# Attention loads on ScalarE's DMA queue, and the last projections tied to the last product

## The chip, the cores and the metric

The kernel runs on one core of a Trainium2 chip. The metric is the device time of one execution in microseconds (us). An execution with the profiler gives the trace that is read here; it shows the engines TensorE (PE; its weight loads are PEld), VectorE (DVE), ScalarE (ACT), GpSimd (POOL) and SyncE (SP). A name with a q behind it, as SPq, is the engine's sequencer, which issues DMAs and waits for semaphores.

## What is computed

Linear attention over 8 batches and 8 heads of 576 rows of 64, then a gated feed-forward layer over the 4608 rows of 512 that come out of it. Inputs and outputs are float32.

```
q_s = softmax of q over its 64 columns
k_s = softmax of k over the 576 rows
kv  = k_s^T v                 per batch and head, 64 x 64
x   = q_s kv                  heads side by side: 4608 x 512
out = ((x @ w_a) * (x @ w_b)) @ w_out     w_a, w_b: 512 x 1536, w_out: 1536 x 512
```

## The kernel before

The 4608 rows are cut into nine chunks of 512 (`T`), numbered `c`. While the feed-forward layer of one chunk runs on TensorE, the attention of the next chunk is done beside it. The program is written in an order that a scheduler then changes: it places each engine's instructions by its own estimate of when they can run, within their dependences. `tc.issue_after(ins)` holds the instructions of a block behind `ins`, where they run on the same engine. On the chip each engine then takes its instructions strictly in order, each waiting for its semaphores; a DMA is issued by an instruction in the order of the engine that issues it, so a DMA that must wait holds up whatever stands behind it there.

The feed-forward layer of a chunk has six steps `i` (`NI`). In each, seven products of 12 matmuls (128x256 outputs, helper `product`) go into the PSUM tiles `kx`, `ky`, `ka` and `kp`: a scheme with seven instead of eight block products, so that some tiles are accumulated on after they have been read. `ky` and `kp` share one bank (tag `k1`), so the product into `kp` must wait until VectorE has read `ky`. ScalarE copies `kx` to `u` (L692), VectorE adds `ky` to it (L693), `ka` after that (L695), and so on, until the gated values `cc` stand there. `g_split` makes two float32r halves of them: ScalarE casts the high one, `gh` (L79), VectorE subtracts for the low one, `gl` (L82). Two such pairs come out of a step, `gh0`/`gl0` and `gh1`/`gl1`, one for each of the twelve (`NF`) parts `f` of w_out. A projection (`project`, L468) multiplies a pair with `wo[f]`: 12 matmuls with 128x512 outputs into the four PSUM tiles `po`. Projections stand in the list `pend` and are run a step later, by `run_pending`, between the products. After the last of a chunk, `store` copies the four `po` tiles to `ot` and sends them out.

The weights of the products come back from DRAM for every chunk after the first two: `get_w` loads `ws` tiles (L165, 512 KB each, eight buffers). The attention of a chunk needs these loads: `k` (L189), `v` (L195), `q` (L277); and, for chunks from 2 on, where q is taken in twice, once for its statistics and once turned, `qtt` (L344) and twice `mr` (L347). `mr` holds the statistics of q, broadcast over partitions; they are written to DRAM as `dq` (L338) and read back. With both there, VectorE adds `mr` to `qtt` (L354), ScalarE takes the exponential (L355) and casts `qh` (L79), VectorE makes `ql` (L82), TensorE multiplies them with `kvh` and `kvl` into `px` (L381), and VectorE multiplies `px` with the other half of `mr` into `xf` (L559). `mr` has two buffers, so the load for the third of four groups waits for that last step of the first.

All DMAs are issued by SyncE. ScalarE issues none. The last lines of the program are

```
    while pend:
        run_pending()
```

and they run the projections that are still open after the last step of the last chunk.

Of the kernel before, what the change touches and what calls it, by code (L numbers as in the profile page):

```python
# [23 lines left out]
A11, S2, S3, S1, A12, S4, A22 = range(7)  # L24
B11, T2, T3, T1, B21, B22, T4 = range(7)
# [4 lines left out]
def linear_attention_then_gated_ffn(  # L30
# [18 lines left out]
    nc = tc.nc  # L49
    B, NP, P, J, _, D = k.shape  # L50
# [3 lines left out]
    NF = 2 * NI  # L54
    T = 512
    H = T // 2
    TT = T // P
    NCH = NT // T
    LATE = NCH - qt_late.shape[0]
# [25 lines left out]
    wo = {}  # L85
# [45 lines left out]
    def split_wo(f):  # L131
        split(wo[f][:, 0], wo[f][:, 1], wo[f][:, 1].bitcast(F32))
# [5 lines left out]
    def split_w(y):  # L138
        w = ws_tile()
        yv = y.rearrange("p (n c f) -> p n c f", n=2, c=2)  # L140
        split(w[:, :, 0], w[:, :, 1], yv)
        return w
# [20 lines left out]
    def get_w(i, op):  # L163
        w = ws_tile()
        nc.sync.dma_start(out=w.bitcast(F32), in_=dw[i, op].bitcast(F32))  # L165
        return w
# [19 lines left out]
    def k_load(b, g, kt=None):  # L186
        if kt is None:
            kt = sb.tile([P, J, 2, D], F32, name="kt")
        nc.sync.dma_start(out=kt, in_=k[b, g])  # L189
        return kt  # L190

    def v_load(b, g, vt=None):
        if vt is None:
            vt = sb.tile([P, J, 2, D + 1], F32, name="vt")
        nc.sync.dma_start(out=vt, in_=v[b, g])  # L195
        return vt

    def kv_soft(b, kt, tags=("at", "at")):
# [75 lines left out]
    def q_load(c, g, qt=None):  # L274
        if qt is None:
            qt = sb.tile([P, TT, 2, D], F32, name="qt")
        nc.sync.dma_start(out=qt, in_=q[c, g])  # L277
        return qt

    def q_soft_first(qt):  # L280
# [60 lines left out]
    def q_turned(c, g, dq):  # L341

        qt = sb.tile([P, T], F32, name="qtt", tag="kt")
        nc.sync.dma_start(out=qt, in_=qt_late[c - LATE, g])  # L344
        mr = sb.tile([P, 2, T], F32, name="mr", bufs=2)
        for h in range(2):
            nc.sync.dma_start(  # L347
                out=mr[h * D:(h + 1) * D].rearrange("d w t -> d (w t)"),
                in_=dq[g, h].unsqueeze(0).broadcast_to([D, 2 * T]),
            )  # L350
        return qt, mr
# [33 lines left out]
    def xo_tile(shape):  # L385
        return sb.tile(shape, F32R, name="xo", bufs=11)
# [56 lines left out]
    def product(pt, w, x, first):  # L443

        for n in range(2):
            i = 0
            for c in range(2):
                for wp, xp in ((0, 0), (0, 1), (1, 0)):
                    nc.tensor.matmul(  # L449
                        pt[:, n], w[:, n, wp, c], x[:, xp, c],  # L450
                        start=(first and n == 0 and i == 0), stop=(i == 5),
                        skip_group_check=True,
                    )
                    i += 1

    def project_first(f, g, po):
        for t in range(TT):
            nc.tensor.matmul(
                po[t], g[:, t * P:(t + 1) * P], wo[f][:, 1].bitcast(F32),
                start=(f == 0), stop=(f == NF - 1),  # L460
            )

    def project(f, ghl, po):
        gh, gl = ghl
        for t in range(TT):
            ts = slice(t * P, (t + 1) * P)
            for i, (a, w) in enumerate(((gh, 0), (gh, 1), (gl, 0))):
                nc.tensor.matmul(  # L468
                    po[t], a[:, ts], wo[f][:, w],
                    start=(f == 0 and i == 0), stop=(f == NF - 1 and i == 2),  # L470
                )

    def store(c, po):
        for t in range(TT):
            ot = sb.tile([P, DM], F32, name="ot", tag="wr", bufs=4)
            if c == NCH - 1:
                nc.scalar.copy(out=ot[:, 0:H], in_=po[t][:, 0:H])
                nc.vector.tensor_copy(out=ot[:, H:], in_=po[t][:, H:])
            else:
                nc.scalar.copy(out=ot, in_=po[t])  # L480
            nc.sync.dma_start(out=out[c * T + t * P:c * T + (t + 1) * P, :], in_=ot)
# [108 lines left out]
    for g in range(NP):  # L590
        kt = const.tile([P, J, P], F32, name=f"kt_first{g}", tag=f"wo{NF - 1 - g}")
        vt = const.tile([P, J, 2, D + 1], F32, name=f"vt_first{g}", tag=f"wo{NF - 5 - g}")
        qt = qts[:, g].rearrange("p n (j h d) -> p (n j) h d", h=2, d=D)
# [14 lines left out]
    for g in range(NP):  # L608
        kt, vt, qt = first[g]
        odd = g % 2  # L610
        kt = kv_soft_t(kt, (("at", "k0"), ("k1", "k2"))[odd])
# [7 lines left out]
        x = xo_tile([P, 2, T])  # L619
# [11 lines left out]
    po = [ps.tile([P, DM], F32, name=f"po{t}") for t in range(TT)]  # L631
    pending = None
    for f in range(NF):
# [10 lines left out]
        ghl = gate_first(f, x0)  # L644
# [3 lines left out]
    pend = [(pending[0], pending[1], 0, po)]  # L648

    def run_pending(last_only=False):  # L650

        if not pend:
            return
        f, ghl, c, po = pend.pop(0)
        (project if c else project_first)(f, ghl, po)
        if f == NF - 1:
            store(c, po)

    last = None
    for c in range(1, NCH):  # L660
        more = c + 1 < NCH
        attend = Spread(attention_tasks(c + 1) if more else [], 3 * NI - 3 - (1 if c == 1 else 0))
        po = None
        x, xo = xo, {}
        for i in range(NI):
            def operand(op):
                if c > 1:
                    return get_w(i, op)
                if op in (A11, A12, A22):
                    return get_w(i, op)  # L670
                w = split_w(sy[i][op])
                put_w(i, op, w)
                return w

            if more and i == NI - 1:
                x_operands(xfs[c + 1], early, xo)
            kx = ps.tile([P, 2, H], F32, name="kx", tag="k0")
            ky = ps.tile([P, 2, H], F32, name="ky", tag="k1")
            ka = ps.tile([P, 2, H], F32, name="ka", tag="k2")
            cc = sb.tile([P, 4, 2, H], F32, name="cc", bufs=1)  # L680
            u2 = sb.tile([P, 2, H], F32, name="u2", bufs=1)
            u3 = sb.tile([P, 2, H], F32, name="u3", bufs=1)
            if c > 1 or i > 0:
                attend(last)
            if c == 1:
                if i + 1 < NI:
                    sy[i + 1] = sums(i + 1)
                split_wo(2 * i)
                split_wo(2 * i + 1)
            product(kx, operand(A11), x[B11], True)  # L690
            product(ky, operand(S2), x[T2], True)
            nc.scalar.copy(out=u2, in_=kx)  # L692
            nc.vector.tensor_tensor(out=u2, in0=ky, in1=u2, op=ALU.add)  # L693
            product(ka, operand(S3), x[T3], True)
            last = nc.vector.tensor_tensor(out=u3, in0=ka, in1=u2, op=ALU.add)  # L695
            if more and i == NI - 1:
                x_operands(xfs[c + 1], late, xo)
            end = c == NCH - 1 and i == NI - 1
            if not end:
                run_pending()  # L700
            attend(last)
            kp = ps.tile([P, 2, H], F32, name="kp", tag="k1")
            product(kp, operand(S1), x[T1], True)
            product(kx, operand(A12), x[B21], False)

            nc.vector.tensor_tensor(out=cc[:, 3], in0=kp, in1=u3, op=ALU.add)  # L706
            nc.scalar.copy(out=cc[:, 0, 0], in_=kx[:, 0])  # L707
            nc.vector.tensor_tensor(out=cc[:, 0, 0], in0=kx[:, 1], in1=cc[:, 0, 0], op=ALU.mult)
            last = nc.vector.tensor_tensor(out=cc[:, 3, 0], in0=cc[:, 3, 0], in1=cc[:, 3, 1], op=ALU.mult)
            if not end:  # L710
                run_pending()
            if po is None:
                po = [ps.tile([P, DM], F32, name=f"po{t}") for t in range(TT)]
            attend(last)
            product(kp, operand(S4), x[B22], False)
            nc.vector.tensor_tensor(out=cc[:, 1], in0=kp, in1=u2, op=ALU.add)  # L716
            nc.vector.tensor_tensor(out=cc[:, 1, 0], in0=cc[:, 1, 0], in1=cc[:, 1, 1], op=ALU.mult)  # L717
            g1 = g_split(2 * i, cc[:, 0:2, 0])
            product(ka, operand(A22), x[T4], False)
            nc.vector.tensor_tensor(out=cc[:, 2], in0=ka, in1=u2, op=ALU.add)  # L720
            last = nc.vector.tensor_tensor(out=cc[:, 2, 0], in0=cc[:, 2, 0], in1=cc[:, 2, 1], op=ALU.mult)
            g2 = g_split(2 * i + 1, cc[:, 2:4, 0])
            pend += [(2 * i, g1, c, po), (2 * i + 1, g2, c, po)]
    while pend:
        run_pending()


# [48 lines left out]
```

## Time and profile before

| | |
|---|---|
| median of 3 runs | 991.0 us (990.97 to 994.56) |
| the profiled execution | 986.57 us, span from first to last instruction 984.5 us |
| mean granted TensorE clock | 0.99 |
| busy: TensorE, its weight loads | 948.7 us (96%), 854.0 us (87%) |
| busy: VectorE, ScalarE, GpSimd | 632.5 (64%), 391.7 (40%), 112.8 us (11%) |
| DMA queue that SyncE issues on | 93600 packets, 282.57 MB, 81.9% of 16 engines' time |
| HBM | read 241.40 MB, written 37.98 MB |

Busy time of TensorE is from each matmul's start to its modelled end. A row of the order of time has its start (us), its length (us), engine, line, operation, tiles and sizes, and in brackets how long the engine had stood idle before it and what released it. Lines are those of the kernel before.

### The profile page before, as it was taken

What the parts mean: (1) busy time and instruction counts of PE and PEld (TensorE: products, weight loads), DVE (VectorE), ACT (ScalarE), POOL (GpSimd) and SP (SyncE); (2) the same over time, 40 slices, a digit from 0 to 9 for tenths busy, and PEclk for the clock granted to TensorE, in tenths of its full rate; (3) what the DMA queues carried; (4) which work ended last, traced back from release to release, by engine and by line L of the source; (5) the groups of instructions that cost most, each with busy time, mean ns of one, the idle gap of its engine ahead of it and who ended that gap; (6) DMA issues with size and microseconds to landing.
All of it is one profiled execution on the core that took longest, in us unless ns stands there. A gap on an engine that the chain in (4) does not pass through costs nothing.

```text
span 984.5 us, 16997 instructions
## 1 busy us (share of the span) xinstructions
PE 948.7 (96%) x6171; PEld 854.0 (87%) x6171; DVE 632.5 (64%) x1259; ACT 391.7 (40%) x1087; POOL 112.8 (11%) x96
## 2 busy tenths in 40 slices
PE   3889999999999999999999999999999999999998
PEld 3757666899999999999999999999999999899996
DVE  7797786988686665656566657565656545653443
ACT  8666675542372325322442335223532263221111
POOL 3245344531000000000000000000000000000000
PEclk9799999999999999999999999999999999999999
DMA  9699858999989967997699779977998679767761
GB/s 346 228 412 397 340 207 293 358 332 303 307 279 338 321 241 280 334 334 259 240 339 328 267 258 341 320 264 252 337 295 295 232 282 288 269 230 262 256 212 46
DMA packets 93682, 283.64 MB, mean 288 GB/s; under 512 B 10848, under 2 KB 11424, under 8 KB 93600
## 3 DMA queue, kind: packets, MB, share of 16 engines
q1 hardware_dynamic: 93600, 282.57, 81.9%
q8 instruction: 49, 0.80, 0.3%
q14 instruction: 33, 0.27, 0.1%
HBM read 241.40 MB, written 37.98 MB: 284 GB/s over the span
## 4 chain that ended last, share of the span: by engine, by line
PE 70%; DMA 6%; DVE 2%; ACT 1%; issue 1%; SPq 0%; DVEq 0%
PE po L468 24%; PE kp L449 12%; PE ka L449 12%; PE kx L449 12%; PE ky L449 6%; DMA mr<-dq 4%; DMA qtt<-in_q_late 2%; PE pk L251 2%; PE px L381 2%; DMA dq<-sst 1%; DVE ws L82 0%; ACT qt L323 0%; SPq L347 0%; DVE ql L82 0%; ACT gh L79 0%
## 5 line engine op out<-in xcount | busy, mean ns | idle before, releaser
L468 PE MATMUL po<-wo_w,gh 128*128 128x512 f32 x768 | 226.5, 394 | 1.0 <-ACT gh L79 1.0
L449 PE MATMUL kx<-xo,ws 128*128 128x256 f32 x1152 | 164.8, 284 | 0.0
L449 PE MATMUL ka<-xo,ws 128*128 128x256 f32 x1152 | 163.1, 285 | 0.9 <-DVE cc L720 0.7
L468 PEld LDWEIGHTS po<-wo_w,gh 128*128 128x128 f32 x768 | 138.8, 189 | 27.3 <-ACT gh L79 1.4
L449 PE MATMUL kp<-xo,ws 128*128 128x256 f32 x1152 | 158.3, 284 | 1.1 <-DVE u L693 1.0
L449 PEld LDWEIGHTS ka<-xo,ws 128*128 128x128 f32 x1152 | 152.1, 192 | 4.5 <-DVE cc L720 0.9
L449 PEld LDWEIGHTS kx<-xo,ws 128*128 128x128 f32 x1152 | 151.9, 191 | 3.5 <-issue 0.5
L449 PEld LDWEIGHTS kp<-xo,ws 128*128 128x128 f32 x1152 | 148.2, 191 | 3.9 <-DVE u L693 1.2
L468 PE MATMUL po<-wo_w,gl 128*128 128x512 f32 x384 | 136.9, 395 | 0.0
L79 ACT CAST gh<-cc 128x512 fp32r<-128x512 f32 x96 | 57.6, 620 | 147.4 <-DVE cc L717 144.1
L716 DVE TENSOR_TENSOR cc<-kp,u 128x512 f32<-128x512 f32 x48 | 33.0, 688 | 89.1 <-PE kp L449 88.8
L323 ACT ACTIVATE qt<-qt,st 128x64 f32<-128x64 f32 x224 | 75.0, 336 | 34.7 <-DVE st L320 30.5
L468 PEld LDWEIGHTS po<-wo_w,gl 128*128 128x128 f32 x384 | 71.2, 188 | 15.3
L449 PE MATMUL ky<-xo,ws 128*128 128x256 f32 x576 | 78.5, 285 | 2.5 <-ACT xo L79 2.1
L426 PE MATMUL pt<-xo,ws 128*128 128x512 f32 x288 | 76.1, 415 | 3.0 <-ACT ga L433 3.0
L449 PEld LDWEIGHTS ky<-xo,ws 128*128 128x128 f32 x576 | 72.9, 192 | 3.2 <-ACT xo L79 2.4
L82 DVE TENSOR_TENSOR gl<-cc,gh 128x512 fp32r<-128x512 f32 x96 | 66.9, 704 | 9.6 <-ACT gh L79 9.4
L426 PEld LDWEIGHTS pt<-xo,ws 128*128 128x128 f32 x288 | 55.0, 194 | 19.3 <-ACT ga L433 4.0
L707 ACT COPY cc<-kx 128x256 f32<-128x256 f32 x48 | 17.7, 370 | 130.8 <-PE kx L449 122.1
L706 DVE TENSOR_TENSOR cc<-kp,u 128x512 f32<-128x512 f32 x48 | 32.9, 685 | 54.8 <-PE kp L449 54.8
L219 POOL PARTITION_ALL_REDUCE mx<-m x20 | 14.1, 704 | 467.2 <-DVE m L205 435.4
L355 ACT ACTIVATE qtt<-qtt 128x512 f32<-128x512 f32 x28 | 17.7, 633 | 103.9 <-DVE qtt L354 77.4
(127 smaller groups left out, 1241.8 us busy)
## 6 DMA issues: line engine op xcount, KB each, us to landing
ws<-dw SPq DMA_DIRECT2D x312, 512.0 KB, 5.2
dw<-ws SPq DMA_DIRECT2D x42, 512.0 KB, 5.0
mr<-dq SPq DMA_DIRECT2D x56, 256.0 KB, 6.5
raw<-in_w_ab SPq DMA_DIRECT2D x24, 512.0 KB, 7.9
out<-ot SPq DMA_DIRECT2D x36, 256.0 KB, 4.8
vt<-in_v SPq DMA_DIRECT2D x28, 325.0 KB, 7.3
qt<-in_q SPq DMA_DIRECT2D x32, 256.0 KB, 5.2
kt<-in_k SPq DMA_DIRECT2D x24, 320.0 KB, 5.8
```

Source lines behind the costliest of these rows:

```text
L79: nc.scalar.copy(out=hi, in_=src)
L82: nc.vector.tensor_tensor(out=lo, in0=src, in1=hi.bitcast(F32), op=ALU.subtract)
L251: nc.tensor.matmul(pk, kt[:, j].rearrange("p h d -> p (h d)"), vt[:, j], start=(j == 0), stop=(j == J - 1),)
L323: nc.scalar.activation(out=qt[:, j, h], in_=qt[:, j, h], func=AF.Exp, bias=st[:, h, 0, j:j + 1], accum_out=st[:, h, 1, j:j + 1],)
L355: nc.scalar.activation(out=qt, in_=qt, func=AF.Exp)
L381: nc.tensor.matmul(px[:, s], w, m[:, s], start=(i == 0), stop=(i == 2))
L426: nc.tensor.matmul(pt, w[:, wp], x[g][:, xp], start=(i == 0), stop=(i == 3 * NP - 1))
L449: nc.tensor.matmul(pt[:, n], w[:, n, wp, c], x[:, xp, c], start=(first and n == 0 and i == 0), stop=(i == 5), skip_group_check=True,)
L468: nc.tensor.matmul(po[t], a[:, ts], wo[f][:, w], start=(f == 0 and i == 0), stop=(f == NF - 1 and i == 2),)
L706: nc.vector.tensor_tensor(out=cc[:, 3], in0=kp, in1=u3, op=ALU.add)
L707: nc.scalar.copy(out=cc[:, 0, 0], in_=kx[:, 0])
L716: nc.vector.tensor_tensor(out=cc[:, 1], in0=kp, in1=u2, op=ALU.add)
```

## The change

The loads of `k` and `v` for batches from 3 on, of `q` for chunks from 2 on, and all of `qtt` and `mr`, are issued by ScalarE instead of SyncE. The projections that are left after the last step are held behind the product `last_product`, the one into `ka`. In the last chunk, the matmuls of the last two projections are held in the order of the four `po` tiles. The four last row copies are each done whole by one engine, VectorE for tiles 0 and 2, ScalarE for 1 and 3; before, ScalarE copied the left half of every tile and VectorE the right.

```diff
     def k_load(b, g, kt=None):
...
-        nc.sync.dma_start(out=kt, in_=k[b, g])
+        (nc.scalar if b > 2 else nc.sync).dma_start(out=kt, in_=k[b, g])
...
     def v_load(b, g, vt=None):
...
-        nc.sync.dma_start(out=vt, in_=v[b, g])
+        (nc.scalar if b > 2 else nc.sync).dma_start(out=vt, in_=v[b, g])
...
     def q_load(c, g, qt=None):
...
-        nc.sync.dma_start(out=qt, in_=q[c, g])
+        (nc.scalar if c > 1 else nc.sync).dma_start(out=qt, in_=q[c, g])
...
     def q_turned(c, g, dq):
         qt = sb.tile([P, T], F32, name="qtt", tag="kt")
-        nc.sync.dma_start(out=qt, in_=qt_late[c - LATE, g])
+        nc.scalar.dma_start(out=qt, in_=qt_late[c - LATE, g])
         mr = sb.tile([P, 2, T], F32, name="mr", bufs=2)
         for h in range(2):
-            nc.sync.dma_start(
+            nc.scalar.dma_start(
...
-    def project(f, ghl, po):
+    def project(f, ghl, po, one_by_one=False):
         gh, gl = ghl
-        for t in range(TT):
...
+        with ExitStack() as in_turn:
+            for t in range(TT):
+                ts = slice(t * P, (t + 1) * P)
+                for i, (a, w) in enumerate(((gh, 0), (gh, 1), (gl, 0))):
+                    ins = nc.tensor.matmul(
+                        po[t], a[:, ts], wo[f][:, w],
+                        start=(f == 0 and i == 0), stop=(f == NF - 1 and i == 2),
+                    )
+                if one_by_one:
+                    in_turn.enter_context(tc.issue_after(ins.ins))

     def store(c, po):
         for t in range(TT):
             ot = sb.tile([P, DM], F32, name="ot", tag="wr", bufs=4)
-            if c == NCH - 1:
-                nc.scalar.copy(out=ot[:, 0:H], in_=po[t][:, 0:H])
-                nc.vector.tensor_copy(out=ot[:, H:], in_=po[t][:, H:])
+            if c == NCH - 1 and t % 2 == 0:
+                nc.vector.tensor_copy(out=ot, in_=po[t])
             else:
                 nc.scalar.copy(out=ot, in_=po[t])
...
-        (project if c else project_first)(f, ghl, po)
+        if c:
+            project(f, ghl, po, c == NCH - 1 and f >= NF - 2)
+        else:
+            project_first(f, ghl, po)
...
-            product(ka, operand(A22), x[T4], False)
+            last_product = product(ka, operand(A22), x[T4], False)
...
-    while pend:
-        run_pending()
+    with tc.issue_after(last_product.ins):
+        while pend:
+            run_pending()
```

(`product` now returns its last matmul.) The scheduler places all of TensorE's, VectorE's and ScalarE's instructions anew from chunk 1 on, so many of them exchange places with a neighbour; the number of matmuls stays the same. Three places matter to what follows.

ScalarE where the turned q of a chunk begins (the boundary that the trace of before has near 713 us; `mr_8063` and `mr_8125` belong to the first two groups). In these rows a number behind a name is that of one buffer's use. Before:

```order
L79 CAST gh0_8031<-cc_7813 128x512
L79 CAST gh1_8051<-cc_7813 128x512
L692 COPY u2_8059<-kx_8055 128x512
L355 ACTIVATE qtt_8061<-qtt_8061 128x512
L79 CAST qh_8130<-qtt_8061 128x512
L707 COPY cc_8058<-kx_8055 128x256
```

And now, where L698 and L713 are the former L692 and L707:

```order
L79 CAST gh0_8031<-cc_7813 128x512
L347 DMA mr_8063<-dq7_7929 64x1024
L79 CAST gh1_8051<-cc_7813 128x512
L344 DMA qtt_8061<-in_q_late 128x512
L347 DMA mr_8063<-dq7_7929 64x1024
L698 COPY u2_8059<-kx_8055 128x512
L347 DMA mr_8125<-dq7_7929 64x1024 x2
L344 DMA qtt_8123<-in_q_late 128x512
L355 ACTIVATE qtt_8061<-qtt_8061 128x512
L79 CAST qh_8130<-qtt_8061 128x512
L344 DMA qtt_8179<-in_q_late 128x512
L713 COPY cc_8058<-kx_8055 128x256
```

Three loads stand ahead of the copy of `u`, three more ahead of the first exponential. On SyncE the same loads stood between the loads of `ws`, which now follow each other there.

ScalarE a little later (near 731 us in the trace of before), where the loads wait for buffers of `mr`. Before:

```order
L79 CAST qh_8186<-qtt_8123 128x512
L79 CAST gh0_8214<-cc_8058 128x512
L79 CAST gh1_8234<-cc_8058 128x512
L692 COPY u2_8242<-kx_8238 128x512
L355 ACTIVATE qtt_8179<-qtt_8179 128x512
L79 CAST xo_8575<-xf_7571 128x512
L79 CAST qh_8251<-qtt_8179 128x512
```

And now:

```order
L79 CAST qh_8186<-qtt_8123 128x512
L347 DMA mr_8181<-dq7_7929 64x1024 x2
L344 DMA qtt_8244<-in_q_late 128x512
L79 CAST gh0_8214<-cc_8058 128x512
L79 CAST gh1_8234<-cc_8058 128x512
L698 COPY u2_8242<-kx_8238 128x512
L347 DMA mr_8246<-dq7_7929 64x1024 x2
L79 CAST xo_8575<-xf_7571 128x512
L355 ACTIVATE qtt_8179<-qtt_8179 128x512
L79 CAST qh_8251<-qtt_8179 128x512
```

Three loads stand ahead of a `gh` cast, two ahead of an exponential, which has also changed places with the cast of `xo`.

TensorE at the end of the program, from the projection of part 8 over that of part 9 to the first matmul of part 10. Before:

```order
L468 MATMUL po3_9930<-wo8_w_1007,gh0_10539 128x512 x2
L468 MATMUL po3_9930<-wo8_w_1007,gl0_10540 128x512
L468 MATMUL po0_9927<-wo9_w_1112,gh1_10559 128x512 x2
L468 MATMUL po0_9927<-wo9_w_1112,gl1_10560 128x512
L468 MATMUL po1_9928<-wo9_w_1112,gh1_10559 128x512 x2
L468 MATMUL po1_9928<-wo9_w_1112,gl1_10560 128x512
L449 MATMUL kp_10614<-xo_9703,ws_10647 128x256 x12
L468 MATMUL po2_9929<-wo9_w_1112,gh1_10559 128x512 x2
L468 MATMUL po2_9929<-wo9_w_1112,gl1_10560 128x512
L468 MATMUL po3_9930<-wo9_w_1112,gh1_10559 128x512 x2
L468 MATMUL po3_9930<-wo9_w_1112,gl1_10560 128x512
L468 MATMUL po0_9927<-wo10_w_1221,gh0_10663 128x512 x2
```

And now (L470 is the former L468):

```order
L470 MATMUL po3_9930<-wo8_w_1007,gh0_10539 128x512 x2
L470 MATMUL po3_9930<-wo8_w_1007,gl0_10540 128x512
L470 MATMUL po0_9927<-wo9_w_1112,gh1_10559 128x512 x2
L470 MATMUL po0_9927<-wo9_w_1112,gl1_10560 128x512
L449 MATMUL kp_10614<-xo_9703,ws_10647 128x256 x12
L470 MATMUL po1_9928<-wo9_w_1112,gh1_10559 128x512 x2
L470 MATMUL po1_9928<-wo9_w_1112,gl1_10560 128x512
L470 MATMUL po2_9929<-wo9_w_1112,gh1_10559 128x512 x2
L470 MATMUL po2_9929<-wo9_w_1112,gl1_10560 128x512
L470 MATMUL po3_9930<-wo9_w_1112,gh1_10559 128x512 x2
L470 MATMUL po3_9930<-wo9_w_1112,gl1_10560 128x512
L470 MATMUL po0_9927<-wo10_w_1221,gh0_10663 128x512 x2
```

The product into `kp` stands ahead of nine matmuls of projection 9 instead of six; the product into `ka` stands ahead of these rows in both. ScalarE's two last casts have changed places: before, `gh1_10683` came ahead of `gh0_10663`, now it follows it.

More of the change, by code (lines that the diff above doesn't have):

```diff
@@ L448, in product @@
                 for wp, xp in ((0, 0), (0, 1), (1, 0)):
-                    nc.tensor.matmul(
+                    ins = nc.tensor.matmul(
                         pt[:, n], w[:, n, wp, c], x[:, xp, c],
@@ L454, in product @@
                     i += 1
+        return ins
     def project_first(f, g, po):
@@ L461, in project_first @@
             )
-    def project(f, ghl, po):
+    def project(f, ghl, po, one_by_one=False):
         gh, gl = ghl
-        for t in range(TT):
[L466 to L471, printed above, removed]
+        with ExitStack() as in_turn:
+            for t in range(TT):
+                ts = slice(t * P, (t + 1) * P)
+                for i, (a, w) in enumerate(((gh, 0), (gh, 1), (gl, 0))):
+                    ins = nc.tensor.matmul(
+                        po[t], a[:, ts], wo[f][:, w],
[3 more added lines that the diff above has]
+                    in_turn.enter_context(tc.issue_after(ins.ins))
     def store(c, po):
```

## The prediction

> **What bounds the kernel now.** I read the page first, then busy time by stretch, then what TensorE waited for, then the waits of SyncE's queue, then the order of time at one chunk boundary and at the end. By stretch (columns: stretch, its length, busy time of each engine with instruction counts, granted TensorE clock, DMA share, GB/s):
>
> ```profile
> 0.00:170.00 170.00, 145.61 (x596) 105.03 (x597) 131.01 (x229) 114.35 (x268) 73.74 (x60) 0.95 0.83 317
> 170.00:225.00 55.00, 51.55 (x358) 47.83 (x357) 49.47 (x90) 26.96 (x94) 23.54 (x16) 0.97 0.94 339
> 225.00:970.00 745.00, 741.97 (x5175) 693.74 (x5174) 447.87 (x934) 247.74 (x720) 15.51 (x21) 1.00 0.82 282
> 970.00:984.50 14.50, 9.57 (x46) 7.37 (x45) 4.11 (x8) 2.63 (x6) 0.00 (x0) 1.00 0.20 73
> ```
>
> TensorE is the bound. The first load that moves is issued shortly before 170 us, so the 24.4 us that TensorE idles up to there stay. From 225 to 970 it idles only 745.00 - 741.97 = 3.03 us, at a granted clock of 1.00; from 170 to 225 it idles 3.45 us. That is all that faster loads could win: 6.5 us. TensorE's waits from 225 to 970 name nearly all of the 3.03 (columns: who waited, for whom, total us, times, longest):
>
> ```profile
> PE px L381 <- DVE ql L82: 1.6, 2, 1.3
> PE kp L449 <- DVE u L693: 1.0, 1, 1.0
> PE px L381 <- ACT qh L79: 0.3, 1, 0.3
> ```
>
> No row has TensorE waiting for a load of weights (`ws`). SyncE's queue, on the other hand, waits all the time (225 to 970):
>
> ```profile
> SPq L165 <- PE kp L449: 153.7, 48, 5.6
> SPq L347 <- DVE xf L559: 29.1, 12, 4.1
> SPq L277 <- ACT qt L323: 26.2, 10, 2.9
> SPq L189 <- DVE ql L82: 23.4, 8, 5.2
> SPq L344 <- DVE ql L82: 17.0, 10, 4.1
> SPq L195 <- DMA mr<-dq: 4.0, 6, 0.9
> ```
>
> The first row says why that costs nothing: the weight loads (L165) wait for TensorE to free a buffer, they are early. The others are waits of the loads that the change moves; until now they held up only SyncE.
>
> **The loads on ScalarE's queue: issue time.** 152 loads move: 28 `q`, 20 `k`, 20 `v`, 28 `qtt` and 56 `mr`. What one issue takes is seen on SyncE alone (min/median/max ns, then issue to landing):
>
> ```profile
> L347 SPq DMA_DIRECT2D mr<-dq x56: 450/587/906, 230.8 to 829.9; - x56
> DMA to landing us min/median/max: 3.8/6.5/9.4
> L344 SPq DMA_DIRECT2D qtt<-in_q_late x28: 327/333/535, 239.3 to 825.5; - x28
> DMA to landing us min/median/max: 3.4/5.9/9.5
> ```
>
> On ScalarE an issue could be hidden in the queue (0) or cost as much as the longest here (0.91). I take the medians: 56 x 0.587 + 96 x 0.333 = 65 us of ScalarE, which is busy 248 of 745 us. What counts is whether it delays an instruction for which TensorE waits. I follow the boundary at 708 to 742, with the rows of the order shown above:
>
> ```profile
> 713.71 1.14 ACT L79 CAST gh<-cc 128x512 fp32r<-128x512 f32 x2 [3.92 <-DVE cc L717]
> 715.10 0.58 ACT L692 COPY u<-kx 128x512 f32<-128x512 f32 x1 [0.24 <-PE kx L449]
> 716.61 0.69 DVE L693 TENSOR_TENSOR u<-ky,u 128x512 f32<-128x512 f32 x1
> 717.78 0.40 PE L468 MATMUL po<-wo_w,gh 128*128 128x512 f32 x1
> 721.68 1.59 PE L449 MATMUL kp<-xo,ws 128*128 128x256 f32 x12
> 722.99 0.63 ACT L355 ACTIVATE qtt<-qtt 128x512 f32<-128x512 f32 x1 [7.30 <-DVE den L257]
> 730.33 0.68 DVE L559 TENSOR_TENSOR xf<-px,mr 128x512 f32<-128x512 f32 x1
> 731.12 0.62 ACT L79 CAST qh<-qtt 128x512 fp32r<-128x512 f32 x1
> 733.55 0.62 ACT L79 CAST gh<-cc 128x512 fp32r<-128x512 f32 x1 [1.82 <-DVE cc L717]
> 736.63 0.68 DVE L559 TENSOR_TENSOR xf<-px,mr 128x512 f32<-128x512 f32 x1
> 736.75 0.63 ACT L355 ACTIVATE qtt<-qtt 128x512 f32<-128x512 f32 x1 [0.37 <-DVE qtt L354]
> 737.87 0.62 ACT L79 CAST qh<-qtt 128x512 fp32r<-128x512 f32 x1
> 740.27 0.37 PE L381 MATMUL px<-qh,kvh 128*128 128x448 f32 x1
> 741.19 0.37 PE L381 MATMUL px<-ql,kvh 128*128 128x448 f32 x1
> ```
>
> First place: the two `gh` casts and the `u` copy get `mr`, `qtt`, `mr` among them, 0.587 + 0.333 + 0.587 = 1.5 us. The copy then ends near 717.0 instead of 715.7. It is needed, by way of VectorE's 0.69 us addition, for `kp` at 721.68 (`kp` takes the bank of `ky`): some 4 us of cover, cost 0. If the cover went, `kp` would be late next. Second place: after the `qh` cast at 731.12 + 0.62 = 731.74 stand two `mr` and one `qtt`, 1.5 us, to 733.25; their release, `xf`, ended at 730.33 + 0.68 = 731.01. The `gh` cast behind them waited for VectorE until 733.55 anyway: cost 0, with 0.3 us to spare. Third place: two `mr` now stand ahead of the next exponential. They are released by `xf` at 737.31, so ScalarE is held from about 736.4 to 738.5; an `xo` cast, the exponential and the `qh` cast follow (0.62 + 0.63 + 0.62), so `qh` is ready near 740.4 instead of 738.49, and `px` wanted it at 740.27. Here the cover is used up: 0.1 us late, and `ql` another 0.69 later just meets its `px` at 741.19. Six chunks have such a boundary: 6 x 0.1 = 0.6 us. Bounds: 0 if the issues are free, 6 x 0.9 = 5 us if each takes 0.9. I take +0.6, from the median rows.
>
> SyncE's queue loses these issues and their waits. The weight loads behind them come earlier, which buys nothing, since no TensorE row waits for one.
>
> **The loads on ScalarE's queue: landing.** `px` waits because `mr` lands late (6.5 us median, 9.4 at most), behind the 512 KB weight loads that were issued ahead of it on the same queue. On a second queue it need not stand behind them. All of it could win the 1.9 us of the two `px` rows; nothing, if the engines are simply shared, as the DMA share of 0.82 to 0.94 suggests; and a loss is possible if the weight loads now land late, but they have all the time in which SyncE waits for `kp`. I take half: -1.0. The Trainium skill is of two minds here. In "DMA: Bandwidth & Descriptors", section "Issuing engines are not separate DMA queues", it says that all issuers run on the same 16 engines and that only the issue time is saved: by that this term would be 0 and the time 990.4. The same page, under "Queues, rings and completion order", says that each engine takes turns between queue rows, packet by packet: by that a load on the second row passes the waiting weight loads, and the term would be the full -1.9, the time 988.5. The trace of before has one queue for all and can't show which.
>
> **The end.** Rows of the last microseconds:
>
> ```profile
> 970.90 1.44 PE kp L449 x12
> 972.17 0.62 PE L468 MATMUL po<-wo_w,gh 128*128 128x512 f32 x2
> 972.37 0.69 DVE L716 TENSOR_TENSOR cc<-kp,u 128x512 f32<-128x512 f32 x1 [3.30 <-PE kp L449]
> 973.10 0.43 DVE L717 TENSOR_TENSOR cc<-cc 128x256 f32<-128x256 f32 x1
> 972.86 0.63 PE L468 MATMUL po<-wo_w,gh 128*128 128x512 f32 x2
> 973.52 1.14 ACT L79 CAST gh<-cc 128x512 fp32r<-128x512 f32 x2 [6.67 <-DVE cc L717]
> 974.72 2.12 PE L468 MATMUL po<-wo_w,gh 128*128 128x512 f32 x8 [0.99 <-ACT gh L79]
> 980.59 0.37 ACT L477 COPY ot<-po 128x256 f32<-128x256 f32 x1 [0.33 <-PE po L468]
> 981.00 0.42 DVE L478 COPY ot<-po 128x256 f32<-128x256 f32 x1 [0.28 <-ACT ot L477]
> ```
>
> The change doesn't quite do what it says: `last_product` is the product into `ka`, and the order has always put `kp` behind it. So `kp` isn't last; 15 projections still stand ahead of it. But nine instead of six now stand behind it. Three projections issue in 972.86 - 972.17 = 0.69 us, one in 0.231. Before, `kp` at 972.17 plus 6 x 0.231 is 973.56, and the next had to wait until 974.72: 1.16 us, because ScalarE cast the `gh` of the last pair first. Now `kp` ends three projections earlier, at 971.48; VectorE's two steps and one cast end 0.69 earlier and one cast (0.62) sooner, near 973.5; the nine projections end at 971.48 + 2.08 = 973.56, so `gh` is there. The third projection needs `gl`, which VectorE finishes 0.69 + 0.03 later, 974.25, against 974.02 wanted: 0.23 us of wait. Gain 1.16 - 0.23 = 0.93. The four row copies: the last took 981.42 - 980.59 = 0.83 through two engines in turn; a whole row takes ScalarE 0.58 (the `u` row above has that shape): 0.25. Bounds of the end, both together: 0.25 (the wait only moves) to 1.41 (it all goes).
>
> **Sum.** +0.6 - 1.0 - 0.93 - 0.25 = -1.6 us. The profiled execution took 986.57 (span 984.5 and 2.07 around it), so its like would take 985.0. The runs shown have a median of 991.0, 4.4 above that execution; the difference is applied to them: 989.4.
>
> **Rivals.** *ScalarE is held (slower).* Its instructions stand in order, so a load that waits holds every `gh` cast and `u` copy behind it. The moved loads' rows above sum to 29.1 + 23.4 + 17.0 + 4.0 = 73.5 us (the 26.2 for `qt` were waits for ScalarE itself, and are gone), with single waits up to 5.2. At the first `gh` use the cover is 717.78 (the projection after 715.10) less 714.33, some 3 us. One wait of 4.1 and one of 5.2 in each of six chunks would cost 6 x (1.1 + 2.2) = 20 us; half of that, 10, gives 1001. It decides from 0.8 us per chunk (5 in six chunks). Against it: SyncE came to those loads early, for want of other work, while ScalarE comes to them behind its own exponentials; in the second place above it finds the release 0.7 us old. For it: ScalarE already stood 7.30 us at the exponential of 722.99, and the third place has no cover left. *The loads land earlier everywhere (faster).* All 6.5 us of idle time after 170 vanish, and the end's 1.2: 983.3. Only the 1.9 us at `px` hang on these loads by name, so I hold this for unlikely. *The queues share, nothing lands sooner.* +0.6 - 1.18: 990.4.
>
> **How the numbers follow.** Forecast (989.4) 0.46, shared queues (990.4) 0.34, ScalarE held (1001) 0.13, all idle gone (983.3) 0.07. A measurement of this kernel can tell about 0.5%, 5 us, from no change. So faster by more has 0.07, within it 0.80, slower 0.13. The likeliest's own range, from the bounds of its terms (-1.41 - 1.9 to +5 - 0.25 around 991.0), is 987.7 to 995.8; the full range reaches a little into the two cases outside it, 986 to 997, and leaves out most of their 0.20.
>
> **What would show it.** Right: TensorE's idle time from 225 to 970 between 1 and 4 us; a median `mr` landing under 6.5 us; ScalarE's issues near 0.33 and 0.59; the 0.99 us row at the last `gh` cast gone, and a last copy of 0.58 us. Wrong: rows of `po` or `kp` waiting for `gh` or `u`, on TensorE, with ScalarE behind a load; or a TensorE row that waits for `ws`.

## The result, and the profile after

The changed kernel takes 997.99 us in the median, the kernel before 991.57 us in the runs beside it; the ratio is 1.0052, with a 95% interval of 1.0032 to 1.0072. It is slower by about 5 us, where 1.6 us of gain had been forecast, and 1 us beyond the range. The profiled execution took 997.99 us, with a span of 995.9 (984.5 before). One of the nine executions of an experiment's kernel below (new order, changed end) was in a slow state, 1560.28 us at a granted clock of 0.56, and is left out of its ratio.

Busy time by stretch, of the kernel after (columns as in the prediction):

```profile
0.00:170.00 170.00, 144.91 (x585) 103.48 (x585) 129.89 (x226) 112.50 (x264) 74.17 (x60) 0.95 0.84 314
170.00:225.00 55.00, 52.26 (x364) 48.98 (x365) 48.07 (x92) 28.95 (x98) 23.52 (x16) 0.97 0.95 350
225.00:970.00 745.00, 733.02 (x5089) 684.04 (x5087) 441.99 (x923) 248.24 (x716) 15.11 (x21) 1.00 0.84 281
970.00:995.90 25.90, 22.17 (x137) 19.19 (x136) 10.98 (x19) 4.40 (x8) 0.00 (x0) 1.00 0.17 62
```

The loss is in the third row: TensorE idles 745.00 - 733.02 = 11.98 us from 225 to 970, 3.03 before; the granted clock of the whole stretch reads 1.00 in both. What it waited for there:

```profile
PE px L381 <- ACT qh L79: 5.6, 7, 1.7
PE kx L449 <- ACT u L698: 4.6, 1, 4.6
PE ky L449 <- DVE cc L722: 1.4, 1, 1.4
PE px L381 <- DVE ql L82: 0.3, 1, 0.3
```

Before, `px` waited 0.3 us for `qh` and 1.6 for `ql`; now 5.6 for `qh`, at seven places. One wait of 4.6 us for the copy `u` is new. Behind both stand the moved loads. The DMA queues (packets, MB, share of 16 engines' time) and the loads' median time from issue to landing, from the list of issues:

```profile
q1 hardware_dynamic: 75296, 239.99, 67.6%
q10 hardware_dynamic: 18304, 42.58, 14.5%
...
mr<-dq ACTq DMA_DIRECT2D x56, 256.0 KB, 8.2
...
qtt<-in_q_late ACTq DMA_DIRECT2D x28, 256.0 KB, 7.3
```

There is a second queue, q10, and on it `mr` lands after 8.2 us instead of 6.5, `qtt` after 7.3 instead of 5.9. The wait for `u` looks like one of another kind, since ScalarE is held by its own loads there. The order of time where TensorE lost its 4.6 us (ACTq is ScalarE's sequencer):

```profile
835.15 1.10 ACTq L347 DMA_DIRECT2D mr<-dq  x2
837.54 0.62 ACT L79 CAST gh<-cc 128x512 fp32r<-128x512 f32 x1 [0.88 <-DVE cc L727]
838.62 4.49 ACTq L347 DMA_DIRECT2D mr<-dq  x2
840.68 1.60 PE L449 MATMUL ky<-xo,ws 128*128 128x256 f32 x12
843.15 0.62 ACT L79 CAST xo<-xf 128x512 fp32r<-128x512 f32 x1 [4.99 <-DMA mr<-dq]
845.01 0.69 DVE L354 TENSOR_TENSOR qtt<-qtt,mr 128x512 f32<-128x512 f32 x1 [5.23 <-DMA mr<-dq]
845.74 0.63 ACT L355 ACTIVATE qtt<-qtt 128x512 f32<-128x512 f32 x1 [1.97 <-DVE qtt L354]
846.27 0.57 ACT L698 COPY u<-kx 128x512 f32<-128x512 f32 x1
846.89 2.50 PE L449 MATMUL kx<-xo,ws 128*128 128x256 f32 x10 [4.62 <-ACT u L698]
```

Two issues that take some 0.5 us each fill 4.49 us here: the second waits for an earlier `mr` load to land, and ScalarE stands idle for 4.99 us ahead of the cast of `xo` behind it. But this isn't what TensorE paid for. The cast ends at 843.77, and ScalarE then stands idle for 1.97 us, because the exponential, which is ahead of the copy of `u` in its order, waits for VectorE's addition. That starts at 845.01, as soon as the second of the two loads issued at 835.15 has landed: it was issued at 835.64 and landed at 844.99, after 9.35 us. So by these rows the copy would have been as late without the held issue; it too waited for a landing. The eight waits of `px` are alike: in each of their groups the addition starts within 0.13 us of a load's landing, and the exponential 0.03 us after the addition. At the wait of `ky`, VectorE stands at such an addition ahead of the step that makes `cc`.

The last row shows one more cost. Ten matmuls of `kx` take 2.50 us where twelve of `ky` took 1.60: from 846.6 to 850.0 the clock record of the trace has 0.50. In the kernel before, no such stretch lies between 225 us and the end.

### The profile page after: what moved, and what is told of

Read it like the earlier page. It is cut to its first block, busy times and chain, and to the rows that moved or that the text cites. A ratio compares the mean times of both kernels' runs of the same rounds, so it can differ in the third digit from the quotient of the medians.

```text
span 995.9 us, 16937 instructions
## 1 busy us (share of the span) xinstructions
PE 952.4 (96%) x6171; PEld 855.7 (86%) x6171; DVE 630.9 (63%) x1257; ACT 394.1 (40%) x1085; POOL 112.8 (11%) x96
## 3 DMA queue, kind: packets, MB, share of 16 engines
q10 hardware_dynamic: 18304, 42.58, 14.5%
## 4 chain that ended last, share of the span: by engine, by line
PE 65%; DMA 18%; DVE 6%; issue 5%; ACT 3%; POOL 2%; SPq 1%; ACTq 0%; DVEq 0%; POOLq 0%
PE po L470 22%; PE ka L449 11%; PE kp L449 11%; PE kx L449 11%; DMA mr<-dq 7%; PE ky L449 6%; DMA qtt<-in_q_late 5%; PE pk L251 2%; POOL wr L103 2%; DMA raw<-in_w_ab 2%; PE px L381 2%; DVE ws L82 1%; DMA wo_raw<-in_w_out 1%; DMA wo_w<-wy 1%; DVE wy L104 1%
## 5 line engine op out<-in xcount | busy, mean ns | idle before, releaser
L470 PE MATMUL po<-wo_w,gh 128*128 128x512 f32 x768 | 228.9, 395 | 1.2 <-ACT gh L79 1.2
L470 PEld LDWEIGHTS po<-wo_w,gh 128*128 128x128 f32 x768 | 139.1, 189 | 27.5 <-ACT gh L79 1.9
L470 PE MATMUL po<-wo_w,gl 128*128 128x512 f32 x384 | 138.6, 396 | 0.0
L470 PEld LDWEIGHTS po<-wo_w,gl 128*128 128x128 f32 x384 | 71.3, 188 | 15.8 <-DVE gl L82 0.4
L426 PEld LDWEIGHTS pt<-xo,ws 128*128 128x128 f32 x288 | 54.9, 194 | 20.2 <-ACT ga L433 4.7
L713 ACT COPY cc<-kx 128x256 f32<-128x256 f32 x48 | 17.8, 371 | 134.6 <-PE kx L449 118.0
```

Source lines behind the costliest of these rows:

```text
L426: nc.tensor.matmul(pt, w[:, wp], x[g][:, xp], start=(i == 0), stop=(i == 3 * NP - 1))
L470: ins = nc.tensor.matmul(po[t], a[:, ts], wo[f][:, w], start=(f == 0 and i == 0), stop=(f == NF - 1 and i == 2),)
```

## The experiments

Three theories. **A**: ScalarE is held in order behind loads that wait. **B**: two queues share the DMA engines, and the loads land later on a queue of their own. **C**: the scheduler's new order of all engines' instructions costs the time. Every ratio is against the kernel before on the same chip, with its 95% interval.

**Parts of the change.** Four kernels: the end alone (all loads on SyncE), and the end with a part of the loads on ScalarE, or with all 152 on GpSimd.

```diff
-        nc.scalar.dma_start(out=qt, in_=qt_late[c - LATE, g])
+        nc.gpsimd.dma_start(out=qt, in_=qt_late[c - LATE, g])   # and so for k, v, q and mr
```

The end alone:

> Only the end of the program is changed (projections behind the product into ka, whole rows copied); all loads stay on SyncE's queue. Theory A (ScalarE stands in order behind loads that wait) and theory B (loads on a second queue land later) both leave only the term of the end, worked out as -0.25 to -1.41 us, so some -1.2 us against the kernel before, ratio 0.9988, with TensorE idle 3 us from 225 to 970 as before and no row of 0.99 us at the last gh cast. Theory C (the new order of instructions, not the loads, costs the time): also about -1.2, since the order changes only at the end here. If the end were the cause of the loss, this kernel would be about 6 us slower than before.

`qtt` and `mr` on ScalarE:

> The end as changed, and only the loads of the turned q (qtt and mr, 84 of the 152) on ScalarE; k, v and q stay on SyncE. A: the waits that held ScalarE were those of mr and qtt, so most of the loss stays: +4 to +7 us against the kernel before, ratio 1.004 to 1.007, TensorE idle 8 to 12 us from 225 to 970, ScalarE rows that wait for a DMA of mr. B: mr again lands at 8 us in the median instead of 6.5, and px waits for qh; about the same time as A.

`k`, `v` and `q` on ScalarE:

> The end as changed, and only the loads of k, v and q (68 of the 152) on ScalarE; qtt and mr stay on SyncE. A: these loads wait for little beside ScalarE itself, so ScalarE is hardly held: -1 to +2 us against the kernel before, ratio 0.999 to 1.002. B: mr is back on the queue of the weight loads and lands near 6.5 us, no row of px that waits for qh: also about -1.2 us. If k, v and q are what costs: +4 us or more.

All of them on GpSimd:

> The changed kernel with the same 152 loads issued by GpSimd instead of ScalarE: a second queue as before, but a load that waits now holds GpSimd, which computes only 15 us from 225 to 970. A: the loss goes; -1 to -3 us against the kernel before, ratio 0.997 to 0.999, TensorE idle 1 to 3 us from 225 to 970. B: mr lands at 8 us or later as on ScalarE's queue and px waits for qh: +5 us, ratio 1.005, TensorE idle about 10 us.

Measured: 0.9994 (0.9972 to 1.0015) for the end alone; 1.0155 (1.0125 to 1.0185) with `qtt` and `mr` on ScalarE; 1.0015 (0.9992 to 1.0037) with `k`, `v` and `q` there; 1.0063 (1.0040 to 1.0085) with all on GpSimd. The end isn't the cause. GpSimd in ScalarE's place loses as much, so A alone can't be the cause. But `qtt` and `mr` alone, 84 of the 152 loads, cost three times what all of them cost, which no theory had foreseen; and each of these kernels also has an order of its own, since the scheduler places everything anew. Until the order is held fixed, they don't tell B from C.

**Order and queue taken apart.** The compute instructions have the same numbers in all these kernels, so the order of one can be imposed on another: each instruction is chained behind its predecessor by an edge that sets the order and adds no wait.

```diff
     with tile.TileContext(nc, schedule_with_timeline_sim=True) as tc:
         linear_attention_then_gated_ffn(tc, *args)
+        in_this_order(tc, nc)
...
+def in_this_order(tc, nc):
+    made = {i.name: i for i in nc.cur_bb.bb.instructions}
...
+            if before is not None and before.engine == i.engine:
+                tc.add_manual_dep(i, before.name, no_wait, reason="order")
+            before = i
```

Old order means that of the kernel before, new order that with the loads on ScalarE. None of the four has the changed end. The new order on ScalarE's queue:

> The move of the 152 loads alone, with the end as before; the scheduler's order of all engines is, but for the end, that of the changed kernel. A (ScalarE is held behind loads), B (loads on a second queue land later) and C (the scheduler's new order of instructions) all give the loss of the changed kernel: +5 to +7 us against the kernel before, ratio 1.005 to 1.007. A ratio at 1.000 would put the loss on the end or on an interplay with it.

The new order, all loads on SyncE:

> The loads stay on SyncE's queue, the end stays as before, but every instruction of TensorE, VectorE, ScalarE and GpSimd is chained in the order that it has with the loads on ScalarE. C: the order costs the time, +5 to +7 us against the kernel before, ratio 1.005 to 1.007. A and B: no second queue and no load on ScalarE, ratio 0.998 to 1.002, mr lands near 6.5 us in the median.

The old order, loads on ScalarE:

> The 152 loads are issued by ScalarE, but every compute instruction of all engines is chained in the order of the kernel before; the end is as before. C: no loss, ratio 0.998 to 1.002. A and B: the loss stays, +5 us or more, ratio 1.005 or more; by B mr lands near 8 us in the median and px waits for qh, by A ScalarE has waits for DMAs and po, kx or kp wait for gh or u.

The old order, loads on GpSimd:

> The same 152 loads from GpSimd's queue, with the order of the kernel before on TensorE, VectorE and ScalarE. It keeps the second queue, and takes ScalarE out of it and the new order too. A: no loss, ratio 0.998 to 1.002. C: no loss. B: mr lands near 8 us, px waits, +4 to +7 us, ratio 1.004 to 1.007.

| | loads on SyncE | on ScalarE | on GpSimd |
|---|---|---|---|
| old order | 1 (the kernel before) | 1.0232 (1.0198 to 1.0266) | 1.0247 (1.0218 to 1.0277) |
| new order | 0.9925 (0.9899 to 0.9951) | 1.0089 (1.0062 to 1.0116) | |

Both were at work, with opposite signs. The queue costs 2.3% in the old order and 1.0089 / 0.9925 = 1.0165, some 16 us, in the new one. The new order by itself gains 0.75%, some 7 us, and that is what kept the change's loss at 0.5%. C is wrong, it has the sign reversed; B's +5 us was far too small.

Old order with ScalarE's queue: the third stretch, the waits of `px`, the landing.

```profile
225.00:970.00 745.00, 724.24 (x5001) 673.22 (x5000) 439.09 (x918) 245.22 (x713) 15.72 (x21) 1.00 0.82 277
...
PE px L381 <- ACT qh L79: 13.3, 11, 3.1
PE px L381 <- DVE ql L82: 4.4, 6, 2.1
...
mr<-dq ACTq DMA_DIRECT2D x56, 256.0 KB, 7.8
```

Old order with GpSimd's queue:

```profile
PE px L381 <- ACT qh L79: 13.6, 10, 4.5
PE px L381 <- DVE ql L82: 5.6, 9, 1.7
...
mr<-dq POOLq DMA_DIRECT2D x56, 256.0 KB, 6.9
...
qtt<-in_q_late POOLq DMA_DIRECT2D x28, 256.0 KB, 7.1
```

New order with SyncE's queue:

```profile
225.00:970.00 745.00, 743.21 (x5184) 695.18 (x5184) 448.24 (x935) 250.24 (x722) 14.63 (x20) 1.00 0.82 281
...
PE po L468 <- ACT gh L79: 1.0, 1, 1.0
PE ky L449 <- DVE cc L716: 0.8, 1, 0.8
...
mr<-dq SPq DMA_DIRECT2D x56, 256.0 KB, 6.5
```

With a second queue nearly all named waits are those of `px`, whoever issues. On GpSimd's queue `mr` lands in the median after 6.9 us, where B had expected some 8; there `qtt`, issued later, is the last of its group to land in 12 of the 28 groups, in 7 before. In the new order on one queue `px` doesn't wait at all.

**The new order with the changed end,** all loads on SyncE:

> All loads on SyncE's queue, the changed end, and every compute instruction chained in the changed kernel's order. If the new order is worth its -8 us wherever the loads are on one queue, and the end its -1.2, this takes -9 us against the kernel before, ratio 0.991, and is the fastest of all. If the gain of the new order was an accident of that one kernel, the ratio is 0.998 to 1.000.

Measured: 984.46 us, 0.9945 (0.9922 to 0.9968). The gain of the new order stands, if smaller than the -9 us expected; that of the end on top of it (0.9925 without) isn't to be seen. Both of these kernels beat the kernel before and the changed one. The lowest ratio is that of the new order alone, 982.64 us in the median where the kernel before took 990.94, but the two intervals overlap.

**Sharing or late issue.** All in the old order. All late loads, those of `ws` too, on GpSimd, so that there is one queue again:

> The order of the kernel before on TensorE, VectorE and ScalarE; the 152 loads and also the 308 loads of ws come from GpSimd's queue, so that they stand in one queue again, only not SyncE's. B (it is the second queue beside that of ws): mr lands near 6.5 us again and the time is that of the kernel before, ratio 0.995 to 1.006. If what costs is that the loads leave SyncE, or GpSimd's way of issuing: +15 us or more, as with the 152 loads alone.

Only `qtt` and `mr` on ScalarE:

> The order of the kernel before; only qtt and mr (84 loads) on ScalarE, k, v and q on SyncE. B: qtt and mr are what px waits for, so most of the +22 us stays: +14 to +24 us, ratio 1.014 to 1.024, mr landing at 7.5 us or later. If the loads of k, v and q were what costs or what crowds the second queue: +2 to +8 us.

All 152 on ScalarE, with half of every `ws` load left out:

> The 152 loads on ScalarE in the order of the kernel before, but each load of ws brings only half of its tile (256 KB instead of 512), and the products use that half twice: the output is another one, the work of all engines is the same. B, as a contest of the two queues for the DMA engines: mr lands below 5.5 us, px hardly waits, and the +22 us go: ratio 0.995 to 1.004. If ScalarE is held by the semaphores of its loads, or the second queue costs by itself: at least half of the loss stays, ratio 1.01 or more.

```diff
-        nc.sync.dma_start(out=w.bitcast(F32), in_=dw[i, op].bitcast(F32))
+        nc.sync.dma_start(out=w[:, 0].bitcast(F32), in_=dw[i, op][:, 0].bitcast(F32))
...
-                        pt[:, n], w[:, n, wp, c], x[:, xp, c],
+                        pt[:, n], w[:, 0, wp, c], x[:, xp, c],
```

One queue, with the loads chained too:

> As the run with all late loads on GpSimd, but the loads too are chained, on GpSimd and on SyncE, in the sequence that SyncE has in the kernel before (28 of 464 had moved, by up to 7 places). B (two queues are what costs): mr lands near 6.5 us and the time comes back to the kernel before, ratio 0.996 to 1.006. If the loss of that run was GpSimd's own issuing (some 0.53 us for each load, and later), it stays: ratio 1.012 or more.

Only the loads of `ws` on GpSimd, the 152 on SyncE:

> The other way round: the 152 loads stay on SyncE and only the 308 loads of ws go to GpSimd's queue; compute and loads are chained in the order of the kernel before. There are two queues again, but the loads of qtt and mr have SyncE for themselves and nothing issues them late. B, sharing alone: mr lands at 7.5 us or later and px waits, +8 us or more, ratio 1.008 or more. If late issue behind compute was what cost: no loss, ratio 0.996 to 1.004, or a gain.

Only `k`, `v` and `q` on ScalarE:

> The order of the kernel before; only k, v and q (68 loads) on ScalarE, qtt and mr on SyncE, the complement of the run with qtt and mr alone. B: mr is back in the queue of ws and lands near 6.7 us; -1 to +5 us, ratio 0.999 to 1.005. If any second queue beside ws costs the same: +15 us or more.

Measured: one queue on GpSimd 1.0177 (1.0153 to 1.0202), and chained 1.0165 (1.0139 to 1.0191); `qtt` and `mr` alone 1.0216 (1.0185 to 1.0246); half the bytes of `ws` 0.9999 (0.9984 to 1.0015); `ws` on GpSimd 1.0308 (1.0279 to 1.0337); `k`, `v`, `q` alone 1.0079 (1.0052 to 1.0107). In the fixed order `qtt` and `mr` alone cost what all 152 loads cost, so the threefold loss above came with the kernels' own orders. `k`, `v` and `q` alone cost more than B's 1.005: they are a second queue beside `ws` too.

To read them together, two times were worked out for each of the 28 groups of `qtt` and `mr`, from the rows of the trace. *Need*: from the issue of the group's second `mr` load to the end of its `qh` cast. *Room*: the matmuls that TensorE has from that issue to the group's first `px`, each at its undisturbed interval (the lower quartile of its shape). A group is short where need exceeds room. The means over the groups, and TensorE's idle time just ahead of `px` from 225 us to 14.5 us before the end, in gaps over 0.3 us:

| order, queue of `qtt`, `mr` / `k`, `v`, `q` / `ws` | ratio | `mr` lands | need | room | short | idle ahead of `px` |
|---|---|---|---|---|---|---|
| old, SP / SP / SP (before) | 1 | 6.5 | 10.55 | 12.36 | 3 | 2.3 |
| new, SP / SP / SP | 0.9925 | 6.5 | 10.86 | 12.75 | 2 | 0 |
| old, ACT / ACT / SP | 1.0232 | 7.8 | 12.17 | 11.72 | 18 | 20.8 |
| old, POOL / POOL / SP | 1.0247 | 6.9 | 12.61 | 12.14 | 18 | 23.1 |
| old, SP / SP / POOL | 1.0308 | 8.0 | 12.10 | 11.72 | 18 | 20.2 |
| old, ACT / SP / SP | 1.0216 | 7.5 | 11.83 | 11.62 | 16 | 19.5 |
| old, SP / ACT / SP | 1.0079 | 6.9 | 11.19 | 12.16 | 9 | 10.3 |
| old, all on POOL, chained | 1.0165 | 6.7 | 10.75 | 11.50 | 9 | 11.2 |
| old, ACT / ACT / SP, half of `ws` | 0.9999 | 5.4 | 10.57 | 13.08 | 2 | 3.3 |
| new, ACT / ACT / SP | 1.0089 | 7.7 | 12.06 | 12.58 | 13 | 9.1 |
| the changed kernel | 1.0052 | 8.2 | 12.27 | 12.44 | 12 | 7.1 |

In the kernel before, the room exceeded the need by 1.8 us in the mean. A second queue beside that of `ws` lengthens the need by 1.3 to 2.1 us, and that takes the cover. That the sharing does it is shown by two runs. With `ws` on GpSimd, SyncE issues nothing but what it issued before, and fewer of it:

```profile
PE px L381 <- ACT qh L79: 13.7, 10, 2.8
PE kp L449 <- DVE cc L706: 6.9, 1, 6.9
PE px L381 <- DVE ql L82: 3.0, 6, 1.6
...
mr<-dq SPq DMA_DIRECT2D x56, 256.0 KB, 8.0
```

And with half the bytes of `ws`, ScalarE still issues all 152 loads, and the loss is gone (this kernel leaves half of every weight tile out, so it shows a time only):

```profile
225.00:970.00 745.00, 741.11 (x5177) 693.46 (x5176) 451.71 (x937) 248.22 (x720) 14.08 (x20) 1.00 0.56 177
...
mr<-dq ACTq DMA_DIRECT2D x56, 256.0 KB, 5.4
```

The packets tell how. In the kernel before, 1.86 MB move in the mean while an `mr` load is in flight: the 1.59 MB of loads in flight ahead of it and its own 0.26; no load issued later lands earlier. In the old order with ScalarE's queue 2.13 MB move, 1.18 on the queue of `ws` and 0.95 on its own. The two queues are served side by side, so some of `ws` that was issued later goes ahead of it; and as `ws` is no longer held behind the attention's loads, more of it is in flight at the issue (1.14 MB instead of 1.02).

Late issue is the smaller part. From the kernel before to the old order on ScalarE, the flight of the second `mr` grew by 1.56 us in the mean, and its issue came 0.64 us later in TensorE's work, which shortens the room. A busy issuer isn't needed for that: with `ws` on GpSimd, where SyncE issues these loads, the room is as short (11.72).

The waits cost more than their own length, since stretches at half the clock follow some of them, as behind the wait for `u` above. From 225 us to 14.5 us before the end, the clock records have none at 0.5 in the kernel before, in the new order on SyncE, with half of `ws` and with `k`, `v`, `q` alone; 3.4 us in the changed kernel, 6.8 in the old order on ScalarE, 13.7 in each of the two runs with all loads on GpSimd, 17.1 with the 152 there, and 27.3 with `ws` on GpSimd. Each such stretch begins during or just after idle time of TensorE of 1 us or more; not every wait of that length has one. With `ws` on GpSimd it shows in the mean of the stretch, 0.98:

```profile
225.00:970.00 745.00, 720.09 (x4920) 668.95 (x4919) 434.98 (x910) 243.38 (x711) 168.86 (x310) 0.98 0.81 273
```

If half the clock means half the work, as the rows behind the wait for `u` suggest, these 27.3 us cost 14 at most by estimate, of the 32.6 (1022.09 - 989.45) that this run loses.

The runs with all loads on one GpSimd queue miss B's expectation in the time, not in the landing (6.8 and 6.7 us). Their rows show another loss, here of the chained one:

```profile
282.75 0.53 POOL L165 DMA_DIRECT2D ws<-dw  x1 [2.75 <-PE po L468]
284.53 1.60 PE L449 MATMUL ka<-xo,ws 128*128 128x256 f32 x12
290.12 0.72 POOL L219 PARTITION_ALL_REDUCE mx<-m  x1 [6.83 <-issue]
290.87 0.83 DVE L222 TENSOR_TENSOR kt<-kt,mx 128x640 f32<-128x640 f32 x1 [8.67 <-POOL mx L219]
291.62 0.68 DVE L706 TENSOR_TENSOR cc<-kp,u 128x512 f32<-128x512 f32 x1
...
PE kp L449 <- DVE cc L706: 6.9, 2, 6.2
```

GpSimd's one compute step of these rows, the reduction `mx`, comes 6.83 us after the load before it; VectorE waits 8.67 us for it, and TensorE for VectorE. No load stands between the two, so it isn't a load that holds `mx`. The trace has two records of GpSimd's own set-up, `MODIFY_POOL_CONFIG`, on the reduction's line, which end at 283.60, 6.52 us ahead of it. In the kernel before they end 54.4 us ahead of the first `mx`, which then starts 0.14 us after its input. With `ws` on GpSimd the distance is 7.21 us, in the unchained run 6.38. So the likely cause is a set-up that had been done early, and now stands in order behind loads that wait for TensorE (2.75 us in the first row); no run shows it by itself. Besides, `mr` is issued later in TensorE's work (a room of 11.50 instead of 12.36), and nine groups are short. The same wait of 6.9 us is in the run with `ws` on GpSimd, whose 3.1% is thus not all sharing; its 20.2 us ahead of `px` are what late landing and late issue explain.

## Why the prediction was wrong, step by step

- **What bounds the kernel** held: TensorE, and the loads matter by way of `px`. What the reading left out is how thin the cover was behind the 1.9 us of visible waits: 3 of 28 groups short, and 1.8 us to spare in the mean.
- **Issue time** was priced about right, 0.587 and 0.333 us against medians of 0.485 (`mr`) and 0.334 (`qtt`) on ScalarE (min/median/max ns):

```profile
L347 ACTq DMA_DIRECT2D mr<-dq x56: 452/485/1143, 231.1 to 842.7; - x56
...
L344 ACTq DMA_DIRECT2D qtt<-in_q_late x28: 330/334/1014, 239.9 to 836.4; - x28
```

  At the boundary that was followed, TensorE lost 0.26 us at the third place, where 0.1 had been forecast, and 0.96 ahead of the next group's `px`; that group's load had landed only 10.2 us after its issue: landing, not issue. A load's issue was taken as its own time and the wait for its buffer; that it can also wait for an earlier load's landing, as in the 4.49 us of two issues at 838 us, was left out, though the row `SPq L195 <- DMA mr<-dq` had shown such waits on SyncE. It cost TensorE nothing there, as the rows above show.
- **Landing is the step that failed.** -1.0 was taken between 0 and -1.9, and a loss was thought possible only if the weight loads landed late. It was the attention's loads that did: 8.2 us instead of 6.5. By the Trainium skill, "DMA: Bandwidth & Descriptors", section "Issuing engines are not separate DMA queues", only issue time is saved by several issuers; here the landings changed too, 6.5 to 8.2 us. The rule of the section "Queues, rings and completion order", that the engines take turns between rows, agrees with the two queues' 1.18 and 0.95 MB; the prediction drew the wrong sign from it. It reckoned with one load that passes a long queue. Here `mr`, `mr` and `qtt` come in bursts and stand behind one another on their own queue: 0.95 MB move there while one load of 0.26 is in flight, and that is less than half of the 2.13 MB that move in all.
- **The new order** had no term at all. "Many exchange places with a neighbour" stood in the description of the change and was priced at nothing; it is worth -0.75%, more than any term of the sum.
- **The end** held. In the kernel after:

```profile
982.53 1.59 PE L449 MATMUL kp<-xo,ws 128*128 128x256 f32 x12
983.96 0.62 PE L470 MATMUL po<-wo_w,gh 128*128 128x512 f32 x2
985.40 1.23 ACT L79 CAST gh<-cc 128x512 fp32r<-128x512 f32 x2 [8.66 <-DVE cc L723]
986.07 0.73 PE L470 MATMUL po<-wo_w,gh 128*128 128x512 f32 x2
992.20 0.58 ACT L483 COPY ot<-po 128x512 f32<-128x512 f32 x1 [0.81 <-PE po L470]
```

  No row of 0.99 us is left, and the last copy takes 0.58. In the same view of the kernel before, `kp` starts at 970.74 (the 970.90 of the prediction is from the chain that ended last):

```profile
970.74 1.59 PE L449 MATMUL kp<-xo,ws 128*128 128x256 f32 x12
```

  From there to the end of the span it was 984.5 - 970.74 = 13.76 us, with six matmuls of projection 9 behind `kp`; with three more, at 0.69 us, it would be 14.45. It is 995.9 - 982.53 = 13.37: a gain of 1.08 where 1.18 was summed. The run of the end alone, 0.9994, can't tell that from nothing.
- **The rivals.** "ScalarE is held" had the sign, but none of TensorE's waits from 225 to 970 can be put down to it: behind each stands a landing, also at the place where ScalarE was held for long. What costs is the sharing, in the opposite direction to the one that the prediction gave it. No rival was allowed to come together with a gain elsewhere, so the size came out right in no case.

The sum as measured: the new order -7 us, the second queue in it +16, the end about -1, which makes +8; the changed kernel shows +5 (3 to 7). Each of the parts has an interval of some 2.6 us to either side, and the two kernels with the new order and ScalarE's queue, with and without the changed end, agree within theirs.

What stays open: how much of the flight's 1.56 us is taking turns, and how much the `ws` loads that are in flight earlier; which of the many exchanges in the new order bring the gain, since its rows show only that `px` no longer waits; and what held GpSimd's reduction.

## What to carry to other kernels

A second DMA queue is no faster lane: in this kernel, with the DMA engines busy 0.8 of the time, it shared them with the first, and loads that had been issued in the order of their need now shared with prefetches that could have waited. An engine that stands at a wait isn't yet the cause: follow each step behind it to what released it. Before a load is moved, work out for each of its users what time is left between its landing and its use, since the visible waits show only the few whose cover is already gone. And where a scheduler places everything anew, measure the new order with the old queues, by itself: here it was the gain in a change that lost.

## What the runs showed of the hardware that was not expected

- A load's time followed the bytes in flight: `mr` landed after 5.4 us with half the `ws` bytes and 7.8 with all of them, on the same queue and in the same order of compute.
- A compute engine that issues loads is held by their waits: ScalarE 4.49 us for two issues, with 4.99 us of idle time ahead of the cast behind them.
- Waits of TensorE were followed by half the clock, in stretches of 3.4 to 10.2 us: ten matmuls in 2.50 us behind a wait of 4.62, twelve in 1.60 ahead of it.
- GpSimd's issues count as its busy time, 0.52 us for an `mr` load, and its loads run on a queue of another kind (`software_dynamic`); the loss was that of ScalarE's queue (1.0247 against 1.0232).
